# Linear attention, top-2 mixture of experts and squared-ReLU MLP in one kernel: reordering the gating of the first tiles, products for warming, k'v in two parts

## The chip, the cores and the metric

One core of a Trainium2 chip runs the whole kernel. The metric is the device time of one execution in microseconds. Engines: TensorE (PE; its weight loads are listed as PEld), VectorE (DVE), ScalarE (ACT), GpSimd (POOL) and SyncE (SP), which issues most DMAs. Every engine works through its own queue in the order of the program. TensorE's clock has two levels, 2.4 and 1.2 GHz; the profile gives the granted clock as a share of full speed, so that 0.5 is the lower level.

## What is computed

Three layers follow one another, all in float32, on 4 batches of 576 tokens (2304 tokens, model width 512):

```python
kv = einsum('bhsd,bhse->bhde', k, v)              # 4 batches, 8 heads, head width 64
o = einsum('bhsd,bhde->bhse', q, kv)
x = o / sqrt(mean(o * o, -1) + 1e-6) * g_norm     # x: 2304 x 512
noisy = x @ w_gate + log1p(exp(x @ w_noise)) * noise      # 8 experts
top2 = the two experts with the largest noisy logits, w = softmax over the two
y[t] = sum over the two: w * (relu(x[t] @ w1[e]) @ w2[e]) # hidden width 1024
h = relu(y @ w_in)
out = (s * h * h + b) @ w_out                     # hidden width 2048
```

## The kernel before, in words

**Front.** The 2304 tokens are 18 tiles of 128 rows; nine tiles belong to batches 0 and 1, nine to batches 2 and 3. They are worked on in ten chunks of two tiles (chunks 4 and 9 have one). The loop over chunks c (lines 739 to 779) interleaves several steps by hand, in this order for each c:

- `att` and `evict`: 16 products of q' with the block-diagonal k'v of the batch (`kvbd`) for each tile, into a PSUM tile with two buffers; ScalarE copies the result to x, a tile with three buffers. The products also give the logits by head, since gate weights are folded into `kvbd` (`mfold_a`, `mfold_b`).
- `squares` (ScalarE) and `inv_rms` of the chunk before (ScalarE's Ln and Exp, then two GpSimd products).
- `kv` of a new batch at c = 0, 3 and 5 (batches 1, 2, 3): 144 products of 64 x 64 and two ScalarE copies `kvc`; `q_tr` of chunk c + 2: eight transposes into one PSUM tile (one buffer) and ScalarE's copy `qT`; `repack` of chunk c + 3; `kv_put`; `mfold_a`.
- `sums` (VectorE's reduction, a GpSimd scaling), then `norm` of the chunk before: four VectorE instructions (L484, L485, L486, L488) that scale x and reduce the logits, and `put_rows`: SP writes the scaled rows to `xs` in DRAM.

**Gating of the first nine tiles.** The generator `gating0` holds it in pieces, and each `next(gating_0)` issues one: (1) `gate_noise`: ScalarE's Exp and Ln, two GpSimd products; (2) `gate_choice` twice: 12 VectorE instructions that pick the two experts; (3) the rank: ten TensorE products (L568, L570); (4) two VectorE sums (L573, L574) and nine one-hots (L548); (5) the table: 18 TensorE products (L554); (6) `idx_e` (L558) and two gathers by GpSimd's queue, which fetch the first 256 rows of expert 0 out of `xs`; (7) `put_x` of each block of 128 rows: four transposes (L380), ScalarE's rounded copy `xh` (L383), VectorE's remainder `xl` (L384), and a copy; then the slots, piece by piece. In the kernel before, (1) and (2) are issued in chunk 6, (3) and (4) in chunk 7, (5) and (6) in chunk 8, (7) in chunk 9, and in each the sums and norm of that chunk stand ahead of or between the pieces.

**Weights.** Every product of the experts and of the MLP is made three times, from high and low halves (fp32r). A unit is a column block of w1 with the row block of w2 that belongs to it. `load_raw` loads one through SP (two buffers); `split_raw` makes the halves: ScalarE w1h (L146), VectorE w1l (L148), ScalarE w2h (L153), GpSimd w2l (L154). `advance(n)` (line 159) splits until n units are done, and keeps the next two on load. In the front it is called with 0 at the end of c = 6, with 1 and 2 in c = 9.

**Main loop.** It goes over (group, unit) steps (lines 1069 to 1085). Group 0 is the 256 rows of expert 0 gathered above, with eight units; then the rest of expert 0, the other experts, and the MLP. Step i issues `l1` of the next unit (12 products, ScalarE's hh, VectorE's hl at L827), then the side work of step i, then `l2` of unit i (products of hh and hl with w2's halves, L846 to L848), then `advance(target(i))`, whose target in group 0 is unit f + 4. Side work of steps 0 to 4 is the gating of the second nine tiles: noise and choice at step 0, the rank, its sums and 9 one-hots at 2, tables at 3 and 4, then the gathers for group 1, which is transposed at step 7. SP also writes zeros to the result table from step 2 on.

**Warming.** `warm(n)` (line 258) issues n products of 512 columns on a constant tile, into a PSUM tile that shares the two buffers of `att`; nothing reads them. The kernel before calls it with 14 at the start and 9 between the two parts of `kv(0)`.

Of the kernel before, what the change touches and what calls it, by code (L numbers as in the profile page):

```python
# [21 lines left out]
def kernel(  # L22
# [136 lines left out]
    def advance(n_split):  # L159
        while split[0] < min(n_split, NU):  # L160
            while loaded[0] < min(split[0] + 2, NU):
                load_raw(loaded[0])
                loaded[0] += 1
            split_raw(split[0])
            split[0] += 1
        while loaded[0] < min(split[0] + 2, NU):
            load_raw(loaded[0])
            loaded[0] += 1
# [49 lines left out]
    def small_ps(shape):  # L218
        p_, tag, bufs = small[0]
        return p_.tile(shape, F32, name="sps", tag=tag, bufs=bufs)  # L220
# [37 lines left out]
    def warm(n):  # L258
        ps = fps.tile([P, KC, P], F32, name="warm", tag="att", bufs=2)
        for _ in range(n):  # L260
            nc.tensor.matmul(ps, lhsT=onesb, rhs=onesb[:, None, :].to_broadcast([P, KC, P]), start=True, stop=True)
# [69 lines left out]
    def kv(b, a0=0, a1=2):  # L331
        K, V = KQV[b, "k"], KQV[b, "v"]
        ps = KVP[b] = KVP.get(b) or [small_ps([P, 2, D]) for _ in range(2)]

        for j in range(KJ):
            for a in range(a0, a1):
                for m in range(2):
                    for i in range(2):
                        r = slice(i * HP, (i + 1) * HP)
                        nc.tensor.matmul(ps[i][m * D:(m + 1) * D, a, :], lhsT=K[r, 2 * a + m, j, :], rhs=V[r, 2 * a + m, j, :],  # L340
                                         start=j == 0 and a == a0, stop=j == KJ - 1 and a == a1 - 1, skip_group_check=True)
        if a1 == 2:
            kvc = pool.tile([P, 2, 2, D], F32, name="kvc", bufs=1)
            for i in range(2):
                nc.scalar.activation(kvc[:, :, i], ps[i], AF.Copy)
            KVP[b] = ps, kvc
# [46 lines left out]
    C0 = NCH // 2 - 1  # L393


    def repack(c):
        if c >= NCH:
            return
        t0, n = CHUNKS[c]
        if n == 2 and TILES[t0][0] > 1:  # L400
            b, j = TILES[t0]
            QC[c] = KQV[b, "q"][:, j:j + 2]
            return
        qc = QC[c] = pool.tile([P, 2, 2, 2, 2, D], F32, name="qc", bufs=2)
        for u in range(n):
            tl = TILES[t0 + u]
            src = KQV[tl[0], "q"][:, :, tl[1], :] if n == 2 else KQV[tl[0] // 2, "qr"]
            src = src.rearrange("p (a m i) d -> p i a m d", a=2, m=2)
            for i in range(2):
                dst = qc[:, u, :, i]  # L410
                if c % 2 or c > C0 + 1:
                    nc.scalar.activation(dst, src[:, i], AF.Copy)
                else:
                    nc.vector.tensor_copy(dst, src[:, i])

    def q_tr(c):
        if c >= NCH:
            return
        t0, n = CHUNKS[c]
        qc = QC.pop(c).rearrange("p u a i m d -> p u (a i) (m d)")  # L420
        pt = fps.tile([P, 2, 4, P], F32, name="qtp", bufs=1)
        for u in range(n):
            for g in range(4):
                nc.tensor.transpose(pt[:, u, g, :], qc[:, u, g, :], ident)
        qT = pool.tile([P, 2, 4, P], F32, name="qT", bufs=2)
        nc.scalar.activation(qT[:, :n], pt[:, :n], AF.Copy)
        QT[c] = qT
# [27 lines left out]
    def sums(c):  # L455
        x, sq = XC[c]
        n = CHUNKS[c][1]
        ss = pool.tile([P, 2, H], F32, name="ss", bufs=2)
        nc.vector.tensor_reduce(ss[:, :n], sq[:, :n], axis=AX, op=OP.add)
        w = pool.tile([P, 2, H], F32, name="iw", bufs=2)  # L460
        nc.gpsimd.tensor_scalar(w[:, :n], ss[:, :n], -0.5 / D, -0.5e-6, op0=OP.mult, op1=OP.add)
        XC[c] = (x, ss, w)
# [15 lines left out]
    def norm(c):  # L478
        if c < 0:
            return  # L480
        x, u, y = XC.pop(c)
        t0, n = CHUNKS[c]
        x, u, y = x[:, :n], u[:, :n], y[:, :n]
        nc.vector.scalar_tensor_tensor(y, u, 1.5, y, op0=OP.add, op1=OP.mult)  # L484
        nc.vector.tensor_mul(x[:, :, :, D:], x[:, :, :, D:], y[:, :, :, None].to_broadcast([P, n, H, W2C]))  # L485
        nc.vector.tensor_reduce(lg[:, t0:t0 + n, :], x[:, :, :, D:].rearrange("p n h c -> p n c h"), axis=AX, op=OP.add)  # L486
        xn = pool.tile([P, 2, H, D], F32, name="xn", bufs=3)[:, :n]
        nc.vector.tensor_mul(xn, x[:, :, :, :D], y[:, :, :, None].to_broadcast([P, n, H, D]))  # L488
        XO.append((t0, n, xn))

    def put_rows():
        if not XO:
            return
        t, n, x = XO.pop(0)
        nc.sync.dma_start(xs[t * P:(t + n) * P, :].rearrange("(n p) d -> p n d", n=n), x.rearrange("p n h d -> p n (h d)"))
# [242 lines left out]
    gating_0 = gating0()  # L738
    for c, (t0, n) in enumerate(CHUNKS):
        new, last = KV_AT.get(c), KV_AT.get(c - 1)  # L740
        for u in range(n):
            att(c, u)
            evict(c, u)
        if c == C0 + 3 or c == C0 + 4:
            next(gating_0)
        if last:
            mfold_b(last)
        squares(c)
        inv_rms(c - 1)
        if c == C0 + 2:  # L750
            next(gating_0)
        if new:
            kv(new)
        if c == 0:
            q_tr(1)
        q_tr(c + 2)
        repack(c + 3)
        if new:
            kv_put(new)
            mfold_a(new)  # L760
        if c == 0:
            load_kv(3)
            load_q(3)
        if c == NCH - 1:
            advance(1)
        sums(c)
        if C0 + 2 <= c <= C0 + 5:
            next(gating_0)
        if c == NCH - 1:
            advance(2)  # L770
        norm(c - 1)
        put_rows()
        if c == NCH - 4:
            advance(0)
    inv_rms(NCH - 1)
# [273 lines left out]
    for n in range(NF2):  # L1049
        i = c_first + n * (c_last - c_first) // (NF2 - 1)  # L1050
# [20 lines left out]
    for i, (g, f) in enumerate(steps):  # L1071
        while nxt[0] < len(steps) and (nxt[0] <= i or nxt[0] == i + 1 and nxt[0] not in LATE_L1):
            s = steps[nxt[0]]
            if s[0] not in X:
                raise RuntimeError("rows of a group come too late")
            l1(*s)
            nxt[0] += 1
        for fn in side.get(i, []):
            fn()
        if i + 1 == NF1:  # L1080
            put_first()
        l2(g, f)
        advance(target(i))
        if f == groups[g][5] - 1:
            finish(g)
# [31 lines left out]
```

## Time and profile before

| | |
|---|---|
| Time, median of 3 runs | 989.93 us (989.27 to 991.34) |
| The profiled execution: time, span | 990.38 us, 988.6 us |
| TensorE, busy | 946.3 us (96%), 5535 products |
| VectorE, ScalarE, GpSimd, busy | 522.8, 395.0, 114.2 us |
| Mean granted clock of TensorE | 0.975 |

The profile is one execution of the program, with starts and lengths of every instruction in microseconds from the start of the span. Busy shares are averages over stages with different limits; what an edit in one stage is worth has to be read from that stage. Matmuls are pipelined and their ends are modelled, so that their lengths overlap. "[3.63 <-DVE g L536]" behind an instruction means that its engine stood idle for 3.63 us before it, until VectorE's instruction of line 536 released it; "issue" is idle time with no releaser in the profile.

### The profile page before, as it was taken

To read this page: it belongs to the slowest core of one execution; us is meant where nothing else is said; L and a number is where in the kernel's file an instruction comes from. 1 tells how busy PE (TensorE), PEld (TensorE's weight loads), DVE (VectorE), ACT (ScalarE), POOL (GpSimd) and SP (SyncE) were. 2 spreads that over 40 slices of the span, in tenths; PEclk is the share of its full clock that TensorE was granted. 3 is DMA by queue.
4 is the path that set the end of the run, shared out by engine and by line. 5 is a ranking of instruction groups with operands and counts; after the bars stand their busy time and mean duration, and the time that the engine had idled before them with its cause. 6 is when DMAs were issued, how large, how long until landed. Compare 5 with 4: busy or idle time off the path is not lost.

```text
span 988.6 us, 14238 instructions
## 1 busy us (share of the span) xinstructions
PE 946.3 (96%) x5535; PEld 820.4 (83%) x5536; DVE 522.8 (53%) x946; ACT 395.0 (40%) x702; POOL 114.2 (12%) x148
## 2 busy tenths in 40 slices
PE   7774999999999999999999999999999999999998
PEld 5773888889999999999999999888788878887886
DVE  1477676544675766767646465444344443434333
ACT  2674234234655555555435343222232232322222
POOL 3014325101000100100000121100110010000000
PEclk8896799999999999999999999999999999999999
DMA  9945667527466574764635542200120021001001
GB/s 294 274 144 168 210 200 251 172 92 252 139 210 226 193 267 157 251 228 141 234 128 192 171 143 71 65 1 11 32 86 1 22 67 41 0 1 43 1 1 42
DMA packets 109722, 129.03 MB, mean 131 GB/s; under 512 B 18224, under 2 KB 74544, under 8 KB 109648
## 3 DMA queue, kind: packets, MB, share of 16 engines
q1 hardware_dynamic: 102224, 108.03, 33.3%
q0 software_dynamic: 6208, 20.00, 6.8%
q8 instruction: 44, 0.72, 0.3%
q14 instruction: 30, 0.25, 0.1%
q10 hardware_dynamic: 1216, 0.03, 0.1%
HBM read 92.91 MB, written 35.13 MB: 130 GB/s over the span
## 4 chain that ended last, share of the span: by engine, by line
PE 76%; DVE 1%; ACT 1%; issue 0%; ACTq 0%
PE ph L823 13%; PE ph L824 13%; PE ph L822 12%; PE y L846 12%; PE y L847 12%; PE y L848 12%; PE sps L380 2%; DVE r L832 0%; DVE xl L384 0%; ACT hh L834 0%; ACT r L831 0%; DVE r L833 0%; DVE hl L835 0%; DVE rows L855 0%; ACT xh L383 0%
## 5 line engine op out<-in xcount | busy, mean ns | idle before, releaser
L823 PE MATMUL ph<-xl,w1h 128*128 128x320 f32 (+3 forms) x832 | 278.8, 335 | 3.0 <-DVE xl L384 2.9
L824 PE MATMUL ph<-xh,w1l 128*128 128x320 f32 (+3 forms) x832 | 278.0, 334 | 2.9 <-DVE w1l L148 2.9
L822 PE MATMUL ph<-xh,w1h 128*128 128x320 f32 (+3 forms) x832 | 278.4, 335 | 2.4 <-ACT xh L383 1.2
L846 PE MATMUL y<-w2h,hh 128*128 128x512 f32 x608 | 243.7, 401 | 0.8 <-PEq L903 0.8
L848 PE MATMUL y<-w2h,hl 128*128 128x512 f32 x608 | 239.5, 394 | 2.0 <-DVE hl L827 2.0
L847 PE MATMUL y<-w2l,hh 128*128 128x512 f32 x608 | 239.3, 394 | 0.0
L822 PEld LDWEIGHTS ph<-xh,w1h 128*128 128x128 f32 x832 | 158.9, 191 | 18.8 <-ACT xh L383 3.4
L823 PEld LDWEIGHTS ph<-xl,w1h 128*128 128x128 f32 x832 | 158.5, 191 | 19.0 <-DVE xl L384 5.4
L824 PEld LDWEIGHTS ph<-xh,w1l 128*128 128x128 f32 x832 | 158.4, 190 | 13.0 <-DVE w1l L148 3.2
L826 ACT ACTIVATE hh<-ph 128x320 fp32r<-128x320 f32 (+2 forms) x128 | 56.0, 437 | 241.2 <-PE ph L824 241.2
L832 DVE SCALAR_TENSOR_TENSOR r<-ph,r 128x512 f32<-128x512 f32 (+1 forms) x80 | 51.0, 637 | 175.9 <-ACT r L831 175.6
L827 DVE SCALAR_TENSOR_TENSOR hl<-ph,hh 128x320 fp32r<-128x320 f32 (+2 forms) x128 | 62.4, 489 | 147.4 <-ACT hh L826 147.4
L848 PEld LDWEIGHTS y<-w2h,hl 128*128 128x128 f32 x608 | 115.2, 189 | 27.7 <-DVE hl L827 2.5
L846 PEld LDWEIGHTS y<-w2h,hh 128*128 128x128 f32 x608 | 115.1, 189 | 22.0 <-ACT xh L383 1.1
L847 PEld LDWEIGHTS y<-w2l,hh 128*128 128x128 f32 x608 | 115.2, 189 | 20.5
L831 ACT ACTIVATE r<-ph 128x512 f32<-128x512 f32 (+1 forms) x80 | 44.4, 554 | 187.9 <-PE ph L824 187.9
L834 ACT ACTIVATE hh<-r 128x512 fp32r<-128x512 f32 (+1 forms) x80 | 47.1, 589 | 101.3 <-DVE r L833 101.3
L835 DVE TENSOR_TENSOR hl<-r,hh 128x512 fp32r<-128x512 f32 (+1 forms) x80 | 51.1, 639 | 52.5 <-ACT hh L834 52.0
L187 POOL DMA_INDIRECT rows<-xs,idx x35 | 34.7, 992 | 314.6 <-PE sps L380 185.8
L187 POOL DMA_INDIRECT rows<-ys,slot_i x36 | 35.0, 972 | 269.1 <-DVE rows L804 134.1
L148 DVE SCALAR_TENSOR_TENSOR w1l<-raw,gcol,w1h 128x512 fp32r<-128x512 f32 x64 | 47.7, 747 | 22.8 <-ACT w1h L146 17.8
L153 ACT ACTIVATE w2h<-raw 128x512 fp32r<-128x512 f32 x80 | 49.6, 620 | 0.7 <-DMA raw<-in_moe_w_dram 0.7
(168 smaller groups left out, 793.9 us busy)
## 6 DMA issues: line engine op xcount, KB each, us to landing
raw<-in_moe_w_dram SPq DMA_DIRECT2D x128, 256.0 KB, 3.8
ys<-rows SPq DMA_DIRECT2D x40, 256.0 KB, 3.8
c_raw<-in_moe_w_in_dram SPq DMA_DIRECT2D x16, 512.0 KB, 6.2
c_raw<-in_moe_w_out_dram SPq DMA_DIRECT2D x16, 512.0 KB, 7.7
wd<-c_fl SPq DMA_DIRECT2D x16, 512.0 KB, 4.8
raw<-wd SPq DMA_DIRECT2D x32, 256.0 KB, 3.0
ys<-zero SPq DMA_DIRECT2D x13, 512.0 KB, 5.3
xs<-xn SPq DMA_DIRECT2D x8, 512.0 KB, 3.5
```

What stands on the lines that cost most here:

```text
L153: nc.scalar.activation(h2, r2, AF.Copy)
L187: nc.gpsimd.indirect_dma_start(out=dst, out_offset=None, in_=src, in_offset=bass.IndirectOffsetOnAxis(ap=icol, axis=0))
L822: nc.tensor.matmul(ps[:, :wd], lhsT=w1h[:, c, :], rhs=xh[:, c, cs], start=c == 0, stop=False)
L823: nc.tensor.matmul(ps[:, :wd], lhsT=w1h[:, c, :], rhs=xl[:, c, cs], start=False, stop=False)
L824: nc.tensor.matmul(ps[:, :wd], lhsT=w1l[:, c, :], rhs=xh[:, c, cs], start=False, stop=c == KC - 1)
L826: nc.scalar.activation(hh[:, cs], ps[:, :wd], AF.Relu)
L827: nc.vector.scalar_tensor_tensor(hl[:, cs], ps[:, :wd], 0.0, hh[:, cs].bitcast(F32), op0=OP.max, op1=OP.subtract)
L832: nc.vector.scalar_tensor_tensor(r[:, :wd], ps[:, :wd], 0.0, r[:, :wd], op0=OP.max, op1=OP.mult)
L835: nc.vector.tensor_sub(hl[:, cs], r[:, :wd], hh[:, cs].bitcast(F32))
L846: nc.tensor.matmul(y, lhsT=hh[:, cs], rhs=w2h, start=f == 0, stop=False)
L847: nc.tensor.matmul(y, lhsT=hh[:, cs], rhs=w2l, start=False, stop=False)
L848: nc.tensor.matmul(y, lhsT=hl[:, cs], rhs=w2h, start=False, stop=f == nf - 1)
```

## The change

In the loop over chunks, the gating's pieces (3) and (4) both stand right behind the att of chunk 7, ahead of `norm` of chunk 5, which moves there from chunk 6; pieces (5) and (6) stand right behind the att of chunk 8, followed by `sums` of chunk 7, which moves there from the end of chunk 7, while `norm` of chunk 6 moves to just ahead of the `sums` of chunk 8. In chunk 9 twelve warming products stand ahead of the split of unit 0, and four behind the transposes of the gathered rows, ahead of the split of unit 1. For batches 1, 2 and 3, `kv` is issued in two halves, with the transposes of q between them. In the first three steps of the main loop `advance(target(i))` stands ahead of the side work too (the call behind `l2` then finds nothing left to do).

```diff
@@ -741,8 +741,16 @@
         for u in range(n):
             att(c, u)
             evict(c, u)
-        if c == C0 + 3 or c == C0 + 4:
+
+        if c == C0 + 3:
             next(gating_0)
+            next(gating_0)
+            norm(c - 2)
+            put_rows()
+        if c == C0 + 4:
+            next(gating_0)
+            next(gating_0)
+            sums(c - 1)
         if last:
             mfold_b(last)
         squares(c)
@@ -750,10 +758,12 @@
         if c == C0 + 2:
             next(gating_0)
         if new:
-            kv(new)
+            kv(new, 0, 1)
         if c == 0:
             q_tr(1)
         q_tr(c + 2)
+        if new:
+            kv(new, 1, 2)
         repack(c + 3)
         if new:
             kv_put(new)
@@ -762,14 +772,22 @@
             load_kv(3)
             load_q(3)
         if c == NCH - 1:
+            warm(12)
             advance(1)
-        sums(c)
-        if C0 + 2 <= c <= C0 + 5:
+        if c != C0 + 3:
+            if c == C0 + 4:
+                norm(c - 2)
+                put_rows()
+            sums(c)
+        if c == C0 + 2:
             next(gating_0)
         if c == NCH - 1:
+            next(gating_0)
+            warm(4)
             advance(2)
-        norm(c - 1)
-        put_rows()
+        if c not in (C0 + 2, C0 + 3):
+            norm(c - 1)
+            put_rows()
         if c == NCH - 4:
             advance(0)
     inv_rms(NCH - 1)
@@ -1075,6 +1093,8 @@
                 raise RuntimeError("rows of a group come too late")
             l1(*s)
             nxt[0] += 1
+        if i < 3:
+            advance(target(i))
         for fn in side.get(i, []):
             fn()
         if i + 1 == NF1:
```

## Rows read from the trace of the kernel before

**Rows 1.** Windows: stretch, length, busy us per engine, TensorE clock, DMA share, GB/s.

```profile
60.00:80.00 20.00, 11.82 (x98) 10.44 (x97) 15.52 (x40) 14.70 (x31) 4.84 (x13) 0.87 0.32 106
80.00:100.00 20.00, 10.41 (x40) 8.23 (x40) 13.65 (x35) 6.26 (x14) 8.10 (x12) 0.59 0.44 145
100.00:127.00 27.00, 26.07 (x188) 22.99 (x189) 16.61 (x44) 8.86 (x18) 8.79 (x7) 0.83 0.73 223
127.00:988.60 861.60, 850.44 (x4426) 739.67 (x4424) 453.78 (x773) 334.39 (x577) 81.50 (x80) 1.00 0.36 118
```

**Rows 2.** Waits of TensorE up to 127 us: total us, times, longest us.

```profile
PE sps L380 <- DMA rows<-xs,idx_e: 8.9, 2, 6.5
...
PE y L848 <- DVE hl L827: 2.0, 1, 2.0
```

**Rows 3.** Timeline of TensorE, 20 to 60 us: start, length, instruction [idle before].

```profile
22.88 2.65 PE L340 MATMUL sps<-v,k 64*64 64x64 f32 x144 [0.33 <-DMA v<-in_v_dram]
...
30.36 0.30 PE L424 MATMUL qtp<-ident,qc 128*128 128x128 f32 x1 [3.92 <-issue]
...
33.97 3.97 PE L437 MATMUL att<-kvbd,qT 128*128 128x160 f32 x16
...
56.58 0.81 PE L340 MATMUL sps<-v,k 64*64 64x64 f32 x38 [1.26 <-issue]
```

**Rows 4.** DMA queues, the half microsecond 27.5 to 28 us: packets, MB, share.

```profile
q8 instruction: 1, 0.02, 13.1%
```

**Rows 5.** Timeline of ScalarE, 57 to 80 us.

```profile
58.45 1.02 ACT L426 ACTIVATE qT<-qtp 128x1024 f32<-128x1024 f32 x1 [0.57 <-PE qtp L424]
...
78.99 0.61 ACT L153 ACTIVATE w2h<-raw 128x512 fp32r<-128x512 f32 x1
```

**Rows 6.** Timeline of VectorE, 64 to 102 us.

```profile
65.04 0.23 DVE L526 TENSOR_REDUCE m_all<-g 128x9 f32<-128x72 f32 x1 [0.59 <-POOL g L513]
...
70.42 1.21 DVE L459 TENSOR_REDUCE ss<-sq 128x16 f32<-128x1024 f32 x1
...
72.03 1.85 DVE L548 TENSOR_SCALAR ohe<-io,early 128x256 f16<-128x256 f16 x9
...
77.22 0.15 DVE L558 TENSOR_SCALAR idx_e<-sps 128x2 int32<-128x2 f32 x1
...
80.24 0.68 DVE L459 TENSOR_REDUCE ss<-sq 128x8 f32<-128x512 f32 x1
...
87.31 0.69 DVE L384 TENSOR_TENSOR xl<-sps,xh 128x512 fp32r<-128x512 f32 x1 [2.78 <-ACT xh L383]
...
88.64 1.25 DVE L484 SCALAR_TENSOR_TENSOR iv<-iu,iv 128x16 f32<-128x16 f32 x1
...
94.78 0.75 DVE L827 SCALAR_TENSOR_TENSOR hl<-ph,hh 128x256 fp32r<-128x256 f32 x2
...
99.82 1.41 DVE L148 SCALAR_TENSOR_TENSOR w1l<-raw,gcol,w1h 128x512 fp32r<-128x512 f32 x2
```

**Rows 7.** Timeline of TensorE, 66 to 102 us.

```profile
68.25 0.48 PE L568 MATMUL sps<-g,onesb 128*128 128x72 bf16 x9 [3.63 <-DVE g L536]
...
72.63 1.71 PE L554 MATMUL sps<-ncen_h,ohe 128*128 128x1 f16 x18
74.27 1.31 PE L437 MATMUL att<-kvbd,qT 128*64 128x160 f32 x16
82.06 1.11 PE L380 MATMUL sps<-ident,rows 128*128 128x128 f32 x4 [6.48 <-DMA rows<-xs,idx_e]
85.55 1.09 PE L380 MATMUL sps<-ident,rows 128*128 128x128 f32 x4 [2.38 <-DMA rows<-xs,idx_e]
...
100.62 0.58 PE L824 MATMUL ph<-xh,w1l 128*128 128x256 f32 x1 [2.91 <-DVE w1l L148]
```

**Rows 8.** Timeline of GpSimd, 76 to 98 us.

```profile
78.32 1.09 POOL L187 DMA_INDIRECT rows<-xs,idx_e  x1 [0.73 <-DVE x L485]
...
94.92 2.51 POOL L154 TENSOR_TENSOR w2l<-raw,w2h 128x512 fp32r<-128x512 f32 x2 [0.38 <-ACT w2h L153]
```

## The prediction

> **What bounds the kernel now.** The busy times by stretch come first, since TensorE works through nearly the whole span: an edit off its path is worth nothing, and one on its path only what TensorE idles or runs slowly. They say where that is [rows 1]: after 127 us 850.44 of 861.6 us are busy at full clock; from 60 to 80 us only 11.82 of 20, from 80 to 100 us 10.41 of 20 at a mean clock of 0.59, from 100 to 127 us the clock is 0.83. The whole stake is the front, up to 127 us. The waits of TensorE there name the largest gap: 8.9 us until the rows of the first two blocks arrive by gather, then 2.0 us in the first l2 for hl [rows 2]. The timelines show what stands in front of each; the rest is read from them.
>
> **Ahead of the gating.** Half of k'v(1) (2.65 us for 144 products, so 1.3 us) now stands behind the transposes of chunks 1 and 2. The stop of 3.92 us before the last transpose of chunk 1 has no releaser ("issue"), and another of 1.26 us lies in k'v(3) [rows 3]; a block of instructions crosses a DMA queue at 27.5 to 28 us [rows 4]. I read both as waits for instructions behind the data loads: each block comes when it comes, and TensorE stops at a fixed count of its program. 348 products stand ahead of the first stop, counted in the timeline from its start; in the new order the 348th is the 63rd of k'v(1)'s second half, so both chunks' transposes and ScalarE's copies of them run before 30.36 us. Left behind it are 9 products (0.2), the k'v copy (0.5) and two transposes (0.6): att of chunk 1 starts near 31.6 instead of 33.97 us, 2.4 us earlier. At c = 3 the split costs: ScalarE takes the copy of the transposed q (1.02 us, its like in [rows 5]) ahead of k'v's, and mfold, which att waits behind, is later by some 0.8. At k'v(3) the second block of instructions is asked for earlier but arrives through the same full queue; I leave 0.6 for that. So 1.0 us is left of 2.4. At c = 5 the copy of the transposed q (58.45 us, 1.02) leaves ScalarE's chain between k'v(3) and the squares of chunk 6 [rows 5]: another 1.0. The first tiles' choice starts 2.0 us earlier. Bounds: 0, if fetches and the loads of the last batch eat it all, to 3.0.
>
> The Trainium skill ("Runtime: NRT & Kernel Launch", section "Instruction fetch mechanics") says that the sequencer streams its blocks beside execution, so that crossing one is mostly hidden; the 3.92 us here disagree. By the page the stop would belong to the transposes and move with them: the early term would shrink to some 0.5 us and the sum below by 1.5.
>
> **From the choice to the index.** VectorE starts the choice at 65.04 and writes idx_e at 77.22 [rows 6]. Between them stand the choice (to 68.2), norm(5) (from there to 70.42, 2.3 us with the overlap), sums(7) (1.2), the first two steps and one-hots (1.85 for the one-hots, 2.3 with the steps from 71.6), norm(6) (2.3) and sums(8) (1.2). The change puts sums(7), norm(6) and sums(8) behind idx_e: 4.6 off, with the overlap of neighbours. One wait is added: the rank products start when the choice ends (68.25 us, 0.48 for nine of ten [rows 7]), and VectorE now stands for them, 0.65 us, where norm(5) covered them. The limit is then TensorE, unchanged in order: from the rank at 68.25 over the transposes and att of chunk 8 to the table's end at 72.63 + 1.71 us is 6.1 us; a table not paced by the one-hots (which end at 73.88) would take less, so 5.2 to 6.1 after the rank's start. Net 2.9 to 3.8, I take 3.2. With the 2.0 from above, idx_e comes 5.2 us earlier, near 72.0.
>
> **From the index to the first products.** The gather starts at 78.32 us, 0.95 after idx_e was written [rows 8]; its rows arrive in TensorE at 82.06 for the first block, and the second block's transposes wait to 85.55 us [rows 7]; the last xl runs 87.31 to 88.00 [rows 6]. SP's queue: the write of chunk 5's rows now comes just before the gather, those of chunks 6 and 7 beside it, as two did before; the loads of weight units 0 and 1 leave before all of them, because SP no longer stands for norm(5) at c = 6. So the second gather should be no slower; the first block took 3.7 us from the first gather's start, the second 7.2, which is at most 6.1 from its own start behind the first's 1.09; between 3.7 and 6.1 I take 5.1, 1.0 less. VectorE sets a floor: the work moved behind idx_e still stands before xl. Its queue was empty at 80.9 us (80.24 + 0.68 [rows 6]); less 2.0, plus the 0.65 wait and two xl of 0.7, xl cannot end before 80.95. Forecast: 88.0 - 5.2 - 1.0 = 81.8 us, 6.2 earlier.
>
> Warming: 12 + 4 products of 512 columns, which step by 0.21 us at 2.4 GHz and by 0.43 at 1.2 GHz (512 columns over either). The twelve start where att of chunk 9 ends (74.27 + 1.31 us before [rows 7], some 2 earlier now, since the table's end moves by that) and end by 78.8 at worst. xh stands behind ScalarE's squares and roots of chunk 9 and the split of unit 0, which ended at 79.60 us [rows 5] and hang on sums(8), which stays near its place: 79.4 whatever the rows do. So the twelve cost nothing; without that cover up to 2. The four stand before the first l1: up to 1.7 late there, hidden by what follows. hl of unit 0 starts at 94.78, 6.8 us after the last xl, behind the split of unit 1, norm(8), norm(9) and slot steps [rows 6]; none of it moves, and TensorE idled 2.0 us for it [rows 2]. So a faster clock in the first two l1 buys nothing either: the wait for hl just grows. It ends 6.2 us earlier.
>
> **In the main loop.** The splits of units 2 and 3 go ahead of the second half's choice. TensorE waited 2.91 us at 100.62 for w1l of unit 2 [rows 7], which stood behind that choice until 99.82 [rows 6]; two w1l take 1.41 us after hl, and that stop goes: -2.9 (bounds -1.5, if the loads of raw weights hold the splits, to -2.9). SP's loads of units 4 and 5 leave earlier with them. Queued behind the splits are now ScalarE's exponent and logarithm of the second half, GpSimd's two noise products (behind two low halves of w2, 2.51 us [rows 8]) and so the choice: it ends some 6 us after hl instead of 5, but its reader, the second rank, stands on TensorE behind l1, l2 and l1 of units 2, 1 and 3, over 6 us at either mix of clock, so this costs nothing; without that cover, 1 us. The products between hl's first (94.78 and 0.4 on) and this stop ran some 2.5 us at the lower level (100.62 less 2.91 less 95.2) and the run-up began anew behind it; now there is one: -1.2 (0 to -1.2). In return the split of unit 5 stands before the second half's one-hots, for which the table products wait: +0.7. Net here -3.4.
>
> The lock of VectorE and GpSimd speaks against it. In the trace iv of norm(8), 16 columns wide, took 1.25 us where xl with 512 columns takes 0.69 [rows 6], beside one of GpSimd's low halves of w2 (two take 2.51 us [rows 8]). The splits of w1 now meet those of units 2 and 3. The Trainium skill ("SBUF — State Buffer", section "Who interferes with whom") says that a VectorE instruction with two SBUF inputs and a GpSimd one that reads SBUF exclude each other for a whole instruction; the 1.25 us agree. By it each of the two w1l could wait 1.26 us, and the sum would lose about 1.3 of its gain.
>
> **The sum.** -6.2 - 3.4 = -9.6 us. The profiled execution took 990.38 us, a span of 988.6 and 1.8 around it; it lies 0.45 above the median of 989.93. Against the median: 980.3 us. Bounds: the early term 2.0 worse, a second gather at 6.1 (1.0), splits held (1.4) and no clock gain (1.2), not all together: some 985.5; the early term at 3.0, xl at its floor (0.9) and no table stop: some 976.5.
>
> **Rivals.** (a) Less than half: the early term is nothing, the second gather as slow as before, VectorE held at the splits by one of GpSimd's 1.26 us: -9.6 + 2.0 + 1.0 + 1.3 = -5.3, or less with a new fetch stop of 1.3 to 3.9: 985 to 988 us. For: two such stops and one lock are in the trace. Against: they cost before, too. 8%. (b) No change, 990: the end hangs on something with its own clock, such as weight loads, and the earlier start is lost in waits later. Against: 850 of 861.6 us busy, DMA share 0.36 after 127 us [rows 1]. 5%. (c) Slower: the group of the first block stays at the lower clock level to its end. At a mean of 0.83, 9.2 of the 27 us from 100 us on are at that level; the other 17.8 would take twice as long, +17.8 - 9.6 = +8.2, 998 us. It decides when over 9.6 of those 17.8 us fall there, which needs new stops between units (w1l waiting for raw weights, one-hots later than the table). For: stops of 2 to 3 us were enough to lower it before. Against: the change takes one of them out. 4%.
>
> **The numbers.** A measurement of this kernel tells 0.2%, 2 us, from no change. The forecast's case, 4.4 to 13.4 us faster, has 83%, (a) 8% and all of it faster: 0.91 faster, 0.05 same, 0.04 slower. The range 976.5 to 985.5 takes in the bounds; outside are most of (a), (b) and (c).
>
> **What would show it.** idx_e near 72; last xl near 82; hl of unit 0 near 88.6; no stop for w1l of unit 2; the product that waited until 100.62 near 91.5; the first transposes of batch 1's chunk with no 3.92 us stop, and a short one in k'v(1)'s second half. Wrong if the last xl ends after 84.5, a new "issue" stop appears ahead of the rank, or the clock from 90 to 120 us is under 0.7.

## The result, and the profile after

The changed kernel takes 981.92 us (median of 4 runs, 979.95 to 983.56) where the kernel before takes 990.04 (989.27 to 991.34): a ratio of 0.9916, 95% interval 0.9891 to 0.994. That is 8.1 us off where 9.6 were forecast, and it lies within the range; the interval lies wholly below 1. The profiled execution took 983.18 us with a span of 981.4, so the two profiles differ by 7.2 us; mean granted clock 0.984 against 0.975.

Lines L822 to L824, L826 and L827, and L846 to L848 of the kernel before are L840 to L842, L844 and L845, and L864 to L866 now. Windows of the changed kernel, with the columns of [rows 1]:

```profile
60.00:80.00 20.00, 15.39 (x114) 12.49 (x114) 14.99 (x40) 13.13 (x28) 5.90 (x14) 0.83 0.43 146
80.00:100.00 20.00, 13.78 (x73) 12.03 (x72) 17.17 (x39) 8.17 (x19) 9.37 (x12) 0.74 0.55 176
100.00:127.00 27.00, 25.52 (x187) 21.75 (x186) 17.30 (x46) 10.21 (x21) 8.14 (x7) 1.00 0.86 260
127.00:981.40 854.40, 843.11 (x4390) 733.00 (x4388) 450.58 (x767) 331.74 (x571) 80.74 (x80) 1.00 0.36 116
```

Against [rows 1] the clock from 80 to 100 us is 0.74 instead of 0.59, from 100 to 127 us 1.00 instead of 0.83. The stretch of the front that was left idle is shorter, and what comes behind the first products of group 1 is as long as before: 861.1 us now (981.4 less 120.26), 861.5 before (988.6 less 127.09). In these two profiles all but 0.4 us of the gain lies in the front, as the prediction had it. TensorE's waits up to 127 us (total, times, longest):

```profile
PE y L866 <- DVE hl L845: 4.1, 1, 4.1
PE sps L568 <- DVE g L536: 3.6, 1, 3.6
...
PE sps L380 <- DMA rows<-xs,idx_e: 0.9, 1, 0.9
...
PE sps L340 <- issue: 0.7, 1, 0.7
PE sps L380 <- DMA rows<-xs,idx_b: 0.7, 1, 0.7
```

Of the 8.9 us for gathered rows [rows 2], 0.9 are left. The wait for hl has grown from 2.0 to 4.1 us and is now the longest here. That it grows with a faster first l1 was forecast; that hl itself is late was not, and the timelines show why. TensorE first:

```profile
29.07 1.16 PE L340 MATMUL sps<-v,k 64*64 64x64 f32 x63
30.96 0.38 PE L340 MATMUL sps<-v,k 64*64 64x64 f32 x9 [0.74 <-issue]
...
32.13 2.34 PE L437 MATMUL att<-kvbd,qT 128*128 128x160 f32 x16
...
48.66 0.76 PE L424 MATMUL qtp<-ident,q 128*128 128x128 f32 x5 [0.70 <-issue]
...
68.39 4.47 PE L437 MATMUL att<-kvbd,qT 128*128 128x160 f32 x16
72.66 0.67 PE L554 MATMUL sps<-ncen_h,ohe 128*128 128x1 f16 x18
...
74.49 2.76 PE L261 MATMUL warm<-onesb 128*128 128x512 bf16 x12
77.35 0.66 PE L380 MATMUL sps<-ident,rows 128*128 128x128 f32 x4
78.90 0.63 PE L380 MATMUL sps<-ident,rows 128*128 128x128 f32 x4 [0.89 <-DMA rows<-xs,idx_e]
...
91.98 0.80 PE L866 MATMUL y<-w2h,hl 128*128 128x512 f32 x1 [4.09 <-DVE hl L845]
```

The stop of 3.92 us ahead of a transpose [rows 3] is gone. What is left of it, 0.74 us, stands behind exactly 63 products of the second half of k'v(1). A second stop without a releaser, 0.70 us, stands in the transposes of chunk 6 at 48.66 us; the one of 1.26 us in k'v(3) [rows 3] is gone. Chunk 1's att starts at 32.13 us (33.97 before), although att of chunk 0, which no edit touches, began at 19.47 instead of 17.94 us in this execution; a part of that is q, which came later (VectorE began to copy it at 15.62 us, 14.87 before). The stop for w1l of unit 2 at 100.62 us [rows 7] has no counterpart. VectorE and GpSimd:

```profile
63.93 0.23 DVE L526 TENSOR_REDUCE m_all<-g 128x9 f32<-128x72 f32 x1 [0.60 <-POOL g L513]
...
67.74 0.24 DVE L573 TENSOR_TENSOR g<-sps,base 128x80 f32<-128x80 f32 x1 [0.65 <-PE sps L570]
...
68.22 1.85 DVE L548 TENSOR_SCALAR ohe<-io,early 128x256 f16<-128x256 f16 x9
...
73.36 0.16 DVE L558 TENSOR_SCALAR idx_e<-sps 128x2 int32<-128x2 f32 x1 [0.99 <-PE sps L554]
...
80.97 0.68 DVE L459 TENSOR_REDUCE ss<-sq 128x8 f32<-128x512 f32 x1
81.57 1.28 DVE L384 TENSOR_TENSOR xl<-sps,xh 128x512 fp32r<-128x512 f32 x2
...
82.83 1.78 DVE L148 SCALAR_TENSOR_TENSOR w1l<-raw,gcol,w1h 128x512 fp32r<-128x512 f32 x1
...
89.13 1.23 DVE L602 TENSOR_SCALAR g<-g 128x18 int32<-128x18 int32 x1
...
90.47 1.13 DVE L605 CAST lh_all<-g 128x36 f32<-128x36 int32 x1
91.52 0.74 DVE L845 SCALAR_TENSOR_TENSOR hl<-ph,hh 128x256 fp32r<-128x256 f32 x2
92.18 1.40 DVE L148 SCALAR_TENSOR_TENSOR w1l<-raw,gcol,w1h 128x512 fp32r<-128x512 f32 x2
...
105.63 0.16 DVE L558 TENSOR_SCALAR tab_b<-sps 128x3 f32<-128x3 f32 x1 [0.39 <-PE sps L554]
```

```profile
73.80 1.09 POOL L187 DMA_INDIRECT rows<-xs,idx_e  x1 [5.76 <-DVE idx_e L558]
75.20 0.99 POOL L187 DMA_INDIRECT rows<-xs,idx_e  x1 [0.30 <-issue]
...
89.06 2.50 POOL L154 TENSOR_TENSOR w2l<-raw,w2h 128x512 fp32r<-128x512 f32 x2 [3.84 <-ACT w2h L153]
```

The reader is to see four things. Between the choice and idx_e only norm of chunk 5 is left. VectorE has no idle time ahead of xl any more (before: 2.78 us [rows 6]); its own queue holds xl, not the rows. Two slot steps of 18 and 36 columns, L602 and L605, take 1.23 and 1.13 us where the kernel before shows 0.25 and 0.18, and they lie inside the 2.50 us that GpSimd spends on two low halves of w2. Then hl, then the splits of units 2 and 3, then the second half's choice. In the kernel before, the same two low halves (94.92 to 97.43 us [rows 8]) run beside that choice instead, and L528, a step of 72 columns, takes 1.20 us there. VectorE before:

```profile
94.32 0.25 DVE L602 TENSOR_SCALAR g<-g 128x18 int32<-128x18 int32 x1
...
94.68 0.18 DVE L605 CAST lh_all<-g 128x36 f32<-128x36 int32 x1
...
96.32 1.20 DVE L528 TENSOR_TENSOR g<-g,rev 128x72 f32<-128x72 f32 x1
```

The front as a chain, each step from the start of one instruction to the start (for xl: the end) of the next one:

| step | before | after | difference | forecast |
|---|---|---|---|---|
| to att of chunk 0 | 17.94 | 19.47 | +1.53 | 0 |
| to the choice (L526) | 47.10 | 44.46 | -2.64 | -2.0 |
| to idx_e | 12.18 | 9.43 | -2.75 | -3.2 |
| to the end of the last xl | 10.78 | 9.49 | -1.29 | -1.0 |
| to hl of unit 0 | 6.78 | 8.67 | **+1.89** | 0 |
| to tab_b, the second half's table | 17.72 | 14.11 | -3.61 | -3.4 |
| to group 1's first product | 14.59 | 14.63 | +0.04 | 0 |
| to the end | 861.51 | 861.14 | -0.37 | 0 |

The sum is -7.2 us; less the late start, which is this execution's own, -8.7.

### The profile page after: what moved, and what is told of

Same layout as the page of the kernel before. It is cut to its first block, busy times and chain, and to the rows that moved or that the text cites. A ratio compares the mean times of both kernels' runs of the same rounds, so it can differ in the third digit from the quotient of the medians.

```text
span 981.4 us, 14268 instructions
## 1 busy us (share of the span) xinstructions
PE 945.3 (96%) x5551; PEld 817.9 (83%) x5552; DVE 523.2 (53%) x946; ACT 395.6 (40%) x702; POOL 115.2 (12%) x148
## 4 chain that ended last, share of the span: by engine, by line
PE 77%; DVE 1%; ACT 1%; issue 0%; ACTq 0%
PE ph L841 13%; PE ph L842 13%; PE ph L840 13%; PE y L864 12%; PE y L865 12%; PE y L866 12%; PE sps L380 2%; DVE r L850 0%; DVE xl L384 0%; ACT hh L852 0%; ACT r L849 0%; DVE r L851 0%; DVE hl L853 0%; DVE rows L873 0%; ACT xh L383 0%
## 5 line engine op out<-in xcount | busy, mean ns | idle before, releaser
L840 PE MATMUL ph<-xh,w1h 128*128 128x320 f32 (+3 forms) x832 | 277.4, 333 | 2.8 <-ACT xh L383 1.6
L842 PE MATMUL ph<-xh,w1l 128*128 128x320 f32 (+3 forms) x832 | 277.5, 333 | 0.0
L864 PE MATMUL y<-w2h,hh 128*128 128x512 f32 x608 | 243.6, 401 | 0.8 <-PEq L921 0.8
L866 PE MATMUL y<-w2h,hl 128*128 128x512 f32 x608 | 238.6, 392 | 4.1 <-DVE hl L845 4.1
L840 PEld LDWEIGHTS ph<-xh,w1h 128*128 128x128 f32 x832 | 157.9, 190 | 19.0 <-ACT xh L383 3.8
L842 PEld LDWEIGHTS ph<-xh,w1l 128*128 128x128 f32 x832 | 157.9, 190 | 9.9
L844 ACT ACTIVATE hh<-ph 128x320 fp32r<-128x320 f32 (+2 forms) x128 | 56.0, 438 | 236.6 <-PE ph L842 230.6
L866 PEld LDWEIGHTS y<-w2h,hl 128*128 128x128 f32 x608 | 114.8, 189 | 29.8 <-DVE hl L845 4.5
L845 DVE SCALAR_TENSOR_TENSOR hl<-ph,hh 128x320 fp32r<-128x320 f32 (+2 forms) x128 | 62.5, 490 | 143.3 <-ACT hh L844 143.3
L864 PEld LDWEIGHTS y<-w2h,hh 128*128 128x128 f32 x608 | 115.0, 189 | 22.0 <-ACT xh L383 1.1
```

The costliest lines, as they stand in the source:

```text
L840: nc.tensor.matmul(ps[:, :wd], lhsT=w1h[:, c, :], rhs=xh[:, c, cs], start=c == 0, stop=False)
L842: nc.tensor.matmul(ps[:, :wd], lhsT=w1l[:, c, :], rhs=xh[:, c, cs], start=False, stop=c == KC - 1)
L844: nc.scalar.activation(hh[:, cs], ps[:, :wd], AF.Relu)
L845: nc.vector.scalar_tensor_tensor(hl[:, cs], ps[:, :wd], 0.0, hh[:, cs].bitcast(F32), op0=OP.max, op1=OP.subtract)
L864: nc.tensor.matmul(y, lhsT=hh[:, cs], rhs=w2h, start=f == 0, stop=False)
L866: nc.tensor.matmul(y, lhsT=hl[:, cs], rhs=w2h, start=False, stop=f == nf - 1)
```

## The experiments

All kernels compute everything; the warming products, which some leave out, are read by nothing. Each set of four ran on one chip of its own, so a time is held against the kernel before on the same chip: 992.20 us (first set, e1 to e4), 992.18 (e5 to e8), 992.64 (e9 to e12). The changed kernel itself ran in the first set (e1) and in the third (e9), not in the second. A ratio is the time over that of the kernel before, with its 95% interval behind it. Beside the times stand chain steps of the profiled executions; "choice to group 1" is the time from the first half's choice to group 1's first product, which the start does not touch (before 62.05 us, after 56.33). Where an edit takes lines out or puts them in, line numbers behind it shift a little; hl is L843 to L845, in e7 L831.

The theory was: the gain is the moved gating, the split of k'v and the early splits; the 1.9 us lost ahead of hl is the mutual lock of VectorE and GpSimd, which the early splits bring into the slot steps. Rivals: that the warming brings the gain through the clock; that hl is late by the longer queue alone.

**e1, the changed kernel again,** as the base of the first set.

> The changed kernel as it is, timed again beside the runs it is compared with. Theory and rivals: 980 to 983.5 us, some 8 us below the kernel before.

982.39 us, ratio 0.9909 (0.9896 to 0.9922). Its profile shows the same chain with the lock on another slot step (144 columns, 0.30 us before):

```profile
84.76 1.37 DVE L594 TENSOR_TENSOR g<-oh_all,g 128x144 f32<-128x144 f32 x1
```

idx_e stands 8.36 us behind the choice, hl 8.67 behind xl, choice to group 1 is 54.85. The 1.07 us between 8.36 and 9.43 are TensorE's clock: att of chunk 8 ran 4.47 us at 0.50 (1.2 GHz) in the profile after, and 3.23 here, where the clock rose to 1.00 midway; in both TensorE had stood idle for 3.6 us for the rank shortly before. The profiles with the new order fall into these two kinds: 8.36 to 8.43 us in six of them (e1, e2, e3, e6, e9, e10), 9.32 to 9.43 in five (after, e4, e5, e11, e12). Chains of different kinds are therefore compared from idx_e on: from there to group 1 it is 46.90 us in the profile after, 46.48 in e1, 46.25 in e9.

**e2, k'v whole again.**

```diff
-            kv(new, 0, 1)
+            kv(new)
...
-        if new:
-            kv(new, 1, 2)
```

> The changed kernel with k'v in one piece again. Theory (the split lets ScalarE copy the transposed q while TensorE stands for instructions, and takes a copy off its chain at c = 5): the choice starts 1 to 2.5 us later against att of chunk 0 than in the changed kernel, the 3.9 us stop before a transpose of chunk 1 is back, and the time is 1 to 2.5 us above the changed kernel's. Rival (the loads of the last batch and the writes of rows set the pace of the front): the stop is back, the choice starts within 0.5 us of the same place, the time is the same within 0.5 us.

985.18 us, 0.9927 (0.9914 to 0.9941): 1.8 us by the ratios, 2.8 by the medians; the interval overlaps e1's, so that the time alone does not show it. The stop is back before the same transpose, with 1.99 us instead of 3.9, since k'v(1) ran later here (24.81 to 28.69 us, 22.88 to 25.53 before):

```profile
31.60 0.30 PE L424 MATMUL qtp<-ident,qc 128*128 128x128 f32 x1 [1.99 <-issue]
```

The choice comes 47.12 us after att of chunk 0, as before (47.10), against 43.35 in e1; from the choice on the chain is e1's (54.83 to group 1). So the split acts on the front up to the choice and nowhere else.

**e3, no warming.**

```diff
-            warm(12)
             advance(1)
...
-            warm(4)
             advance(2)
```

> The changed kernel without the 16 warming products. Theory (the wait for hl hides whatever the clock does to the first two l1): l1 of units 0 and 1 run at the lower clock and end about 2 us later, the 4.1 us wait for hl shrinks by as much, hl starts within 0.3 us of the same place, the time is the same within 0.7 us. Rival (the clock that the warming holds up carries into group 0): 2 to 3 us slower.

982.69 us, 0.9911 (0.9896 to 0.9925): the sixteen products bring nothing and cost nothing; choice to group 1 is 54.83 against 54.85. They do move something: the first products run at the lower clock level, so hh and ScalarE's splits behind it come later, and the lock falls behind hl instead of ahead of it. VectorE in e3:

```profile
87.14 0.18 DVE L605 CAST lh_all<-g 128x36 f32<-128x36 int32 x1
87.24 0.75 DVE L843 SCALAR_TENSOR_TENSOR hl<-ph,hh 128x256 fp32r<-128x256 f32 x2
87.91 3.06 DVE L148 SCALAR_TENSOR_TENSOR w1l<-raw,gcol,w1h 128x512 fp32r<-128x512 f32 x2
```

hl stands 6.77 us behind xl, as before, which was not expected ("within 0.3 us of the same place"), and two w1l take 3.06 us instead of 1.40. The lock costs 1.9 us ahead of hl with the warming and 1.7 us behind it without; the chain comes out even.

**e4, the early splits undone.**

```diff
-        if i < 3:
-            advance(target(i))
```

> The changed kernel with the splits of units 2 and 3 back behind the side work. Theory (the early splits let GpSimd's low halves of units 2 and 3 lock the slot steps ahead of hl): the slot steps L602 and L605 take 0.2 us again instead of 1.2 and 1.1, hl starts 1.5 to 2 us earlier, the stop for w1l of unit 2 is back with 2 to 4 us, the time is 1 to 2 us above the changed kernel's. Rival (no lock; the early splits are pure gain): hl starts in the same place, the time is 2.9 to 4 us above.

984.69 us, 0.9928 (0.9915 to 0.9941): 1.9 us lost by the ratios, with an interval that just overlaps e1's. The stop for w1l is back, TensorE of e4:

```profile
87.90 0.79 PE L866 MATMUL y<-w2h,hl 128*128 128x512 f32 x1 [2.25 <-DVE hl L845]
93.27 0.58 PE L842 MATMUL ph<-xh,w1l 128*128 128x256 f32 x1 [2.88 <-DVE w1l L148]
```

hl comes 6.80 us behind xl, and hl to tab_b is 17.71 us, before's 17.72. The early splits thus take 3.6 us off behind hl and bring 1.9 back ahead of it. The mean clock in the 20 us from hl on is 0.68, as in the kernel before, against 0.83 in e1 and 0.86 in the profile after.

**e5, the low halves of units 2 and 3 on VectorE.** If the lock holds hl, it goes with GpSimd's work.

```diff
-        low_engine[0].tensor_sub(l2, r2, h2.bitcast(F32))
+        (nc.vector if u in (2, 3) else low_engine[0]).tensor_sub(l2, r2, h2.bitcast(F32))
```

> The changed kernel with the low halves of w2 of units 2 and 3 made by VectorE, behind their w1l, instead of by GpSimd. Theory (lock): the slot steps ahead of hl take 0.2 to 0.3 us each, hl starts 6.8 us after the last xl instead of 8.7, VectorE pays 1.4 us for the two low halves behind hl; the ratio to the kernel before falls by 0.0005 to 0.002 against the changed kernel's. Rival (the slot steps are long for another reason): 8.7 us stay, the ratio rises by up to 0.0015.

```profile
87.65 0.18 DVE L602 TENSOR_SCALAR g<-g 128x18 int32<-128x18 int32 x1
...
87.93 0.18 DVE L605 CAST lh_all<-g 128x36 f32<-128x36 int32 x1
88.03 0.75 DVE L845 SCALAR_TENSOR_TENSOR hl<-ph,hh 128x256 fp32r<-128x256 f32 x2
88.69 0.74 DVE L148 SCALAR_TENSOR_TENSOR w1l<-raw,gcol,w1h 128x512 fp32r<-128x512 f32 x1
89.36 0.83 DVE L154 TENSOR_TENSOR w2l<-raw,w2h 128x512 fp32r<-128x512 f32 x1
```

The slot steps are back at 0.18 us and hl at 6.76 us behind xl: with early splits, warming and the queue otherwise as they were, the lock alone is the 1.9 us. VectorE now does the two low halves itself (0.83 and 0.68 us) ahead of the second choice, but that takes nothing back: hl to tab_b is 13.38 us (13.55 in e1), and TensorE does not wait for the choice. Choice to group 1 is 53.90 us, only 0.95 under e1, because idx_e comes 9.41 us behind the choice here, as in the profile after, and not 8.36; from idx_e to group 1 it is 44.49 us, 2.0 under e1. The time does not show it: 982.46 us, 0.9909 (0.9892 to 0.9925), the ratio of e1; an interval of 3.3 us, on a chip without a run of the changed kernel, cannot tell whether the 2.0 us remain. As a diagnosis the run is clear, as a remedy it is open.

**e6, the slot steps behind the first half's l2.** The slots are not needed until group 1; if they only stand in front of hl, moving them gives their time back. The rival: they then stand in front of the second half's one-hots.

```diff
     put_rows()
-    run(gating_0)
...
+    at(1, lambda: run(gating_0))
```

> The changed kernel with the slot steps of the first tiles moved from the end of the front to step 1 of the main loop, behind the first hl. Theory (VectorE's queue between the last xl and hl sets when the first l2 goes on): hl starts 5.4 to 6.7 us after the last xl instead of 8.7, TensorE's stop there falls from 4 or 5 us to 1 to 3, the time is 2 to 3 us below the changed kernel's, the ratio near 0.988. Rival (what comes next holds the same end: the second half's choice, its one-hots, the rows of group 1): the stop shrinks, the time by less than 0.7 us.

982.82 us, 0.9916 (0.9899 to 0.9934): the rival. hl came 5.40 us behind xl, the earliest so far, but TensorE then waited for one-hots:

```profile
99.43 0.65 PE L554 MATMUL sps<-ncen_h,ohe 128*128 128x1 f16 x3 [2.63 <-DVE ohe L548]
101.12 1.81 PE L554 MATMUL sps<-ncen_h,ohe 128*128 128x1 f16 x24 [1.05 <-DVE ohe L548]
```

tab_b stands 40.06 us behind the choice, as in e1: hl to tab_b took 16.82 us instead of 13.55.

**e7, the old order of the gating with the rest of the change.** The hunks on `gating_0`, `norm` and `sums` of the diff are left out; k'v in two halves, warming and early splits stay.

> The kernel before with everything of the change but the order of the gating: k'v in two parts, warming, early splits. Theory: idx_e comes 12.2 us after the choice's start, as before, the gather's rows are waited for again (5 us or more at the first transposes), the last xl comes 21 to 23 us after the choice's start instead of 18.9 and the time is 3 to 5 us above the changed kernel's, ratio 0.994 to 0.996. Rival (the gain is that of k'v and the splits; VectorE's queue would hold xl anyway): under 1.5 us above, ratio under 0.9925.

988.50 us, 0.9966 (0.9953 to 0.9979): 5.7 us of the change's 9 are the gating's order, somewhat more than the 3 to 5 expected. The run undoes all its hunks at once; what each is worth by itself is not shown. Choice to idx_e is 12.20 us and choice to the last xl 23.01, before's 12.18 and 22.96, and the waits for both blocks' rows are back (3.83 us for the first); the second:

```profile
83.16 1.09 PE L380 MATMUL sps<-ident,rows 128*128 128x128 f32 x4 [2.37 <-DMA rows<-xs,idx_e]
```

hl stands 8.60 us behind xl here too: the lock comes ahead of hl with the early splits, not with the gating.

**e8, the early splits alone on the kernel before.**

```diff
+        if i < 3:
+            advance(target(i))
         for fn in side.get(i, []):
             fn()
```

> The kernel before with the early splits alone. Theory: the 2.9 us stop for w1l of unit 2 goes; low halves of w2 may stretch steps ahead of hl by up to 1.9 us; 1 to 3 us below the kernel before, ratio 0.997 to 0.999. Rival (the stop is only moved): a new wait of 2 us or more ahead of the rank's products, ratio 0.9995 or more.

989.72 us, 0.9975 (0.9965 to 0.9985): 2.5 us, about what e4 lost. Without warming the lock falls on the two w1l behind hl (3.10 us), hl at 6.72. The rival's wait ahead of the rank's products did come, but it costs less than the stop that went:

```profile
104.86 0.38 PE L568 MATMUL sps<-g,onesb 128*128 128x72 bf16 x9 [2.22 <-DVE g L536]
```

**e9, the changed kernel a third time,** as the base of the third set.

> The changed kernel once more, for comparison on the same chip: ratio 0.990 to 0.992.

984.34 us (979.78 to 986.19), 0.992 (0.9905 to 0.9936).

**e10, the slot steps behind the second table.** The small tiles of the slots get names of their own, so that the second half need not wait for them.

```diff
-        return gp.tile(shape, dt, name=f"g{n[0]}", bufs=1)
+        return gp.tile(shape, dt, name=f"g{n[0]}_{g if n[0] > 4 else 0}", bufs=1)
...
-    run(gating_0)
...
+    at(5, lambda: run(gating_0))
     at(5, lambda: run(gate_slots(1)))
```

> The changed kernel with the first tiles' slot steps at step 5 of the main loop, behind the second half's one-hots, in tiles of their own. Theory (VectorE's queue from the last xl to the second half's one-hots holds the table products, and through them group 0's end): hl starts 5.4 to 6 us after the last xl, tab_b comes 38 to 39 us after the first choice's start instead of 40, the time is 1 to 2 us below the changed kernel's. Rival (the choice of the second half waits for GpSimd's low halves and gives it all back): tab_b at 40, the time within 0.7 us.

982.20 us (978.08 to 984.26), 0.9889 (0.9871 to 0.9907): 2.1 us under e9 by the medians, intervals that overlap, so not clear by itself. In the profile hl is early (5.49) but VectorE stands idle for the second half's noise, which waits on GpSimd behind two low halves of 3.55 us:

```profile
91.17 0.23 DVE L526 TENSOR_REDUCE m_all<-g 128x9 f32<-128x72 f32 x1 [1.91 <-POOL g L513]
```

TensorE then waits 4.28 us for that choice. tab_b is at 39.86 behind the first choice: nearly all that was gained at hl is lost here.

**e11, e10 with the second half's noise ahead of the early splits.**

```diff
+        if i == 0:
+            side[0].pop(0)()
         if i < 3:
             advance(target(i))
```

> As before it, and the noise of the second half ahead of the splits of units 2 and 3. Theory: the choice follows w1l of unit 3 without a wait for GpSimd, tab_b comes 36 to 38 us after the first choice's start, the time is 2 to 4 us below the changed kernel's, ratio 0.987 to 0.989. Rival (ScalarE waits for the last norm ahead of w1h of units 2 and 3, and l1 of unit 2 for that; or the rows of group 1 are next): under 1 us below.

980.25 us (979.2 to 984.69), 0.9882 (0.9864 to 0.9901), an interval just below e9's. tab_b is at 38.59, with idx_e at 9.32; from idx_e on it is 29.3 us, 31.4 in e10. The profiled execution itself took 867.1 us behind group 1's start where the others of its set took 862.7 to 864.4; why is open.

**e12, e11 with the early split in the first two steps only,** so that unit 5's split does not stand before the second half's one-hots.

```diff
-        if i < 3:
+        if i < 2:
```

> As before it, with the early split for the first two steps only, so that unit 5 is split behind the one-hots. Theory: the one-hots start 0.7 us earlier, tab_b as much, the time 0 to 0.7 us below the last one's. Rival (GpSimd's low half locks or l1 of unit 5 waits): 0 to 1 us above it.

980.00 us (979.2 to 981.58), 0.9875 (0.9857 to 0.9894). It beats both kernels: the interval lies below that of the changed kernel on the same chip (0.9905 to 0.9936), by 4.3 us in the medians. tab_b is at 37.93, choice to group 1 53.38 us, 1.5 under e1; idx_e comes 9.43 us behind the choice here, too, and from idx_e to group 1 it is 43.95 us, 2.5 under e1 and 2.3 under e9. TensorE's waits from hl on:

```profile
87.66 0.51 PE L865 MATMUL y<-w2h,hl 128*128 128x512 f32 x1 [0.84 <-DVE hl L844]
94.47 0.38 PE L568 MATMUL sps<-g,onesb 128*128 128x72 bf16 x9 [1.33 <-DVE g L536]
...
113.63 1.39 PE L380 MATMUL sps<-ident,rows 128*128 128x128 f32 x8 [1.32 <-DMA rows<-xs,idx_b]
```

4.09 us for hl have become 0.84; next are the second choice (1.33) and the rows of group 1 (1.32). Against the changed kernel's other ratios (0.9909 in e1, 0.9916 in the result) the gain is 3.4 to 4.1 us. The 2.3 to 2.5 us in the chain from idx_e on account for over half of it; where the rest comes from, one profile of each cannot tell.

## Why the prediction was right, and where it was not

By the ratios and a base of 992 us, undoing the parts one at a time costs 5.7 us (order of the gating), 1.8 (k'v whole), 1.9 (early splits) and 0.2 (warming); their sum of 9.6 is about the whole gain in e1, 9.0. The parts that the prediction named carry it. By the times alone only the first is clear of e1's interval; those of k'v and of the early splits rest on the chain.

**The early term,** -2.0, was right in its mechanism and somewhat too small. The stop sits where the count of the 348th product puts it, at the 63rd of the second half (the trace has 16 att products for chunk 0 as a whole, not for each of its tiles). An instruction block starts to cross its queue at 28.41 us (27.82 before), and the stop ends at 30.96 us (30.36 before): both 0.6 later, while att of chunk 0 is 1.5 later. The other profiles agree: all but e10's, which has no such stop, have it behind the 348th product, 3.92, 1.99 and 4.27 us long without the split (before, e2, e8), 0.40 to 1.53 us with it, and it ends 2.4 to 2.65 us after the start of such a block. So the end of the stop goes with the block, and what changed is how much work stands ahead of it. That data loads hold the block up, as the prediction read it, is not shown. The DMA queues of the changed kernel from 28 to 28.5 us, with the columns of [rows 4]:

```profile
q8 instruction: 1, 0.02, 13.7%
```

Att of chunk 1 starts 3.4 us earlier against att of chunk 0 (12.66 us instead of 16.03) where 2.4 were forecast. The loss of 0.8 us that was forecast at c = 3 did not come: att of chunk 4 starts 4.1 us earlier against att of chunk 0 (26.25 us instead of 30.33), although TensorE waits 0.71 us for k'v's copy. Then 0.7 us goes to the second stop without a releaser, at 48.66 us: a new "issue" stop ahead of the rank, which the prediction had named as a sign of being wrong. It stands behind the 600th product, the one of 1.26 us that it replaces behind the 727th, and e1 has it too (0.71 us). At c = 5, where a gain of 1.0 was forecast, 1.0 is lost to two waits for q's loads (0.52 and 0.80 us); e1 has neither and gains 3.75 us up to the choice. The choice came 2.64 us earlier in the profile after, and 2.35 to 4.8 in the other runs with the split; without it 47.10 and 47.12 us after att of chunk 0, but 45.86 in e8, so that a part of the spread is the execution's own. The Trainium skill ("Runtime: NRT & Kernel Launch", section "Instruction fetch mechanics") has the fetch mostly hidden, by which the stop would have moved with the transposes; the trace disagrees: it stayed with the block.

**From the choice to the index,** -3.2: -2.75 in this profile, just outside the bounds of 2.9 and 3.8, and -3.8 in e1, at the upper one. TensorE paces it, as forecast: VectorE waits 0.65 us for the rank and 0.99 for the table. Which of the two values comes depends on the clock of att of chunk 8, which the prediction took from one profile.

**The gather,** -1.0: -1.29. The second block's rows were transposed 3.7 us after their gather's issue (75.20 to 78.90 us), at the low end of the bounds of 3.7 to 6.1. VectorE's queue then was the floor that the prediction named; the last xl ended at 82.85 us, not 81.8, in an execution that started 1.5 us late, so 0.5 earlier than forecast against its start. (The range's lower end of 976.5 does not follow from the terms named for it: an early term of 3.0, xl at its floor and no +0.7 for the table make 977.7.)

**From xl to hl** the prediction failed: "none of it moves". hl came at 91.52 us instead of 88.6, 1.5 of it the late start. The 6.8 us were taken to be fixed, since no instruction in VectorE's queue there changes. But GpSimd's queue beside it did. The early splits bring ScalarE's halves of units 2 and 3, and with them GpSimd's low halves, to 89 us, and the warming (by an earlier hh) adds its part: the low halves meet the slot steps, and hl comes 1.9 us later. Shown by three runs that change only one side: without early splits 6.80 us (e4), without warming 6.77 (e3), with the low halves off GpSimd 6.76 (e5), against 8.67. The prediction knew of the lock and looked for it at w1l of units 2 and 3, one place too late in the queue; there it did strike in e3 (3.06 us for two) and e8 (3.10). The 1.25 us of [rows 6] had already shown that a 16-column step is hit as hard as a large one, and the "one lock" that it counted in the trace missed a second, L528's 1.20 us in the kernel before: the lock of these two low halves was not brought in by the change but moved, from behind hl to ahead of it. The steps that were hit ahead of hl took 1.13 to 1.39 us at 8 to 144 columns, about one low half each. The rule in the Trainium skill ("SBUF — State Buffer", section "Who interferes with whom") has, beside instructions with two SBUF inputs, also copy, cast and tensor_scalar in a two-port mode; the trace agrees in that L583 (COPY), L605 (CAST) and L602 (TENSOR_SCALAR) were hit as L484 and L594 were, with two inputs; the mode itself no run shows. By it the sum would have lost 1.3 us; the trace lost 1.9.

**In the main loop,** -3.4: -3.61. The stop for w1l of unit 2 (2.91 us) is gone, and with it 1.33 us by which L527 and L528 of the choice ahead of it were long. The clock is 1.00 from 100 to 127 us in this profile (0.83 before, 0.94 in e1 and e9); in the 20 us from hl on it is 0.86, 0.83 in e1 and e9, 0.68 before. Undoing the early splits gives the stop back and the 0.68 (e4). How much of the -3.61 is the clock's is not separated.

**Warming**, 0: 0.2 us in the time (e3), nothing in the chain. hl held TensorE either way (5.3 us in e1, 1.05 in e3).

So in the chain the 1.9 us ahead of hl, less the 1.0 us by which the other terms together came out larger, make -8.7 of the -9.6; that the sum came so near is in part luck, since half of the missed term was made good by others. The medians give -8.1, the ratios of e1 and e9 -9.0 and -7.9. Rivals (a) to (c) did not come: the gain is over half, none of it is lost behind 127 us, and the clock from 100 to 127 us did not fall below that of before. Where hl was brought forward by moving the slot steps (e6, e10) the next wait was near; e11 and e12, which took the next ones too, lie below the changed kernel of their set.

## What to carry to other kernels

When a step is hoisted, list the instructions that it issues on every engine and ask what each of them will now run beside; a step that stays in place can still grow, and where two engines exclude each other a short instruction of a critical queue can lose as much as a long one (0.16 us became 1.28). Count program positions where a trace shows a stop with no releaser: work put ahead of the position is done during the stop. And shortening one wait in a chain of in-order queues pays only as far as the next one, so look for the next two before moving anything.

## What the runs showed of the hardware that was not expected

- A step of 8 columns on VectorE (L583, 0.16 us alone) took 1.28 or 1.29 us beside one of GpSimd's low halves, in e1, e4, e5 and e10; GpSimd can pay too: two low halves take 2.50 us in the profile after, and 3.55 in e10.
- One and the same program starts att of chunk 0 anywhere from 17.97 to 19.47 us (the changed kernel in three profiles), and its granted clock in att of chunk 8 differs from execution to execution: 0.50 throughout in one, rising to 1.00 midway in the two others, worth 1.07 us at idx_e. Runs of one kernel spread by 3 to 6 us.
- The part behind group 1's first product took 861.1 us in the profile after, and 863.0 and 863.1 us for the same kernel in e1 and e9, on two chips.
